# Moving the zeroing of the sine weights' first row (columns 0 to 1023) ahead of the mixing matrices' loads

## The chip, the cores and the metric

The kernel runs on one core of a Trainium2 chip. The time is that of the device for one execution, in microseconds (us). The program drives five engines, each with its own list of instructions that it works off in order: TensorE (PE, with a separate row PEld for its weight loads), VectorE (DVE), ScalarE (ACT), GpSimd (POOL) and SyncE (SP). SP computes nothing in this kernel: it issues transfers (DMAs), which then run on 16 DMA engines. An instruction that needs something from another engine, or from a transfer, waits on a semaphore, and everything behind it on its own engine waits too.

## The reference

The input x has 8 batches of 3008 positions with 256 values each. The reference takes the discrete Fourier transform over the positions and over the values, keeps the real part, and sends each of the 24064 rows through a small network with the activation h * sigmoid(1.702 h):

```
X = np.fft.fft(x, axis=1)
X = np.fft.fft(X, axis=2)
x = X.real.astype(np.float32).reshape(B * S, D)      # 24064 x 256
h = x @ w_in                                          # 256 x 2048
g = h * (1.0 / (1.0 + np.exp(-1.702 * h)))
return g @ w_out                                      # 2048 x 256
```

All of it is float32.

## The kernel before

**The mathematics.** 3008 is 47 times 64, so the transform over positions is done in two stages: 47 points (for batch 0 `mix_first`, later `mix1`) and then 64 points (`stage2`). The transform over the values is not done on the data at all. It is multiplied into w_in: `fold_w` makes a cosine version `wcs[0]` and a sine version `wcs[1]` of w_in, each 128 rows by 2048 columns. The sine of row 0 would be zero, and its place is used for something else: row 0 of `wcs[1]` first holds the weights of the highest frequency (the "Nyquist" row), which `first_row` copies into the small tiles `af1` and `af2`, 512 columns at a time.

**The slots.** The main loop has 384 slots and three more to drain it (loop variable `t`, line 978). Sixteen slots make a block, three blocks a batch, eight batches the run. A slot computes 256 of the hidden units for 256 positions and their mirror images. The first eight slots (`NP` is 8) form their products with `hidden(t)`, and `rows(t)` corrects the result for what row 0 of `wcs[1]` contributes. From slot 8 on another scheme is used: `middle(t)` (line 584) fills a PSUM bank with the Nyquist part, `begin(t)` adds the cosine product and `begin(t, 1)` the sine product into the same bank, and this is right only if row 0 of `wcs[1]` is zero by then. Slot t uses 256 of the 2048 columns, chosen by the last three bits of t: slots 0 to 3 and 8 to 11 use columns 0 to 1023, slots 4 to 7 and 12 to 15 the others.

**The zeroing.** `no_row(c0)` (line 497) is one DMA of 4 KB: it copies 1024 zeros from a table in DRAM into row 0 of `wcs[1]`, columns c0 to c0 + 1023. It is called twice: `no_row(0)` after `hidden(4)` in slot 4, and `no_row(1024)` after `hidden(7)` in slot 7. It may not overwrite the row before the last of the earlier products has read it: for columns 0 to 1023 that is `hidden(3)`.

**What SP has in its list around it.** SP's order is the order in which the Python code emits the calls. Work that is hung on a slot with `at(t, ...)` is emitted at the end of that slot. In slots 0 and 1 SP gets the last two loads of the raw w_out (`load_out`, line 397, 1 MB each). At the end of slot 3 come `load_matrices` (line 324, four loads of the 47-point matrices into `w1`), `turn` (lines 196 and 192, three DMAs that write the reversed half of the next x to the DRAM tensor `Xr1`), and `load_x` (line 205, eight loads of the next x into `xt`, half of them from `Xr1`). Then follow `no_row(0)` and `no_row(1024)`. The next things in the list are a small DMA to DRAM in slot 9 (line 383) and the first stores of results in slot 10 (line 815).

SP's DMAs signal on eight semaphores in turn, so a DMA is issued only when the one eight places ahead of it has landed. One DMA more or less in the list therefore changes which earlier DMA a later one waits for.

**The slots just after the first eight.** Slot 8 is the first in which `begin(t, 1)` reads the zeroed row. PE's order from there is: `begin(8, 1)`, a part of `product(5)`, `begin(9)`, the rest of `product(5)`, then `stage2` of block 1 (line 360), `begin(9, 1)`, a part of `product(6)`, `begin(10)`. The banks are shared: the results of slots 8 and 10 lie in bank `b0`, and `stage2` in slot 8 uses `b0` between the two. So `stage2` on PE waits until DVE has read slot 8's bank (`backward(8)`, line 557), and `middle(10)` on ACT waits until DVE has transposed `stage2`'s result out of `b0` (line 366). Two further groups of work lie in these slots: `small_weights(0)` to `(3)` on DVE (line 687, four instructions each, in slots 7 to 10), and on POOL the last `finish_out` (line 465), `differences` (line 475, four instructions each, in slots 5 to 8) and `sums` (lines 614 and 615). On DVE `small_weights(1)` stands in slot 8 after `backward(8)` and before the transposes of line 366. On ACT `forward(t)` is line 599, `doubled(t)` line 596 and `activate_back(t)` line 606.

From slot 11 on POOL also does `fold1` (lines 218 to 231) on the x that `load_x` brought.

Of the kernel before, what the change touches and what calls it, by code (L numbers as in the profile page):

```python
# [112 lines left out]
def kernel(ctx: ExitStack, tc, x, w_in, w_out, tab1, tab2, out):  # L113
# [255 lines left out]
    def nyquist(b, blk):  # L369

        nb = nbt[b, blk] = pqp.tile([128, 512], F32, tag="nb", name="nb")
        row = pqt[b, blk][0:1, 1, :]
        if (b, blk) != (0, 0):
            nc.sync.dma_start(out=nb[:], in_=view(Nd, (b * NBLK + blk) * 512, [0, 128], [1, 512]))
            return
        ps = bank("psn")
        halves(ps[:], ones[:], row, start=True, stop=True)
        nc.scalar.copy(nb[:], ps[:])
# [39 lines left out]
    def low_up(key, lo=0, n=1024):  # L418

        nc.scalar.activation(pre[key][2][:, lo:lo + n].bitcast(F32), raw[key][:, lo:lo + n, 0], ACTF.Copy, scale=2.0 ** -29,  # L420
                             bias=2.0 ** 23)

    def low_down(key, lo=0, n=1024):
        r = pre[key][2][:, lo:lo + n]
        nc.scalar.activation(r, r.bitcast(F32), ACTF.Copy, bias=-2.0 ** 23)

    def bounds(key, end=True):
        prepare(key)
        squares(key, nc.scalar)
        clamp(key)  # L430
        low_up(key)
        if end:
            low_down(key)
# [43 lines left out]
    def fold_w(n):  # L477
        ps = [bank("psw") for _ in range(2)]
        for i in range(2):
            for cs in range(2):  # L480
                halves(ps[cs][:], cd[:, i, cs, :], wst[n][:, i, :], start=(i == 0), stop=(i == 1))
        for cs in range(2):

            nc.scalar.copy(wcs[cs][:, n * 512:(n + 1) * 512].rearrange("p (f c) -> p f c", f=4),
                           free(ps[cs][:], 0, [1, 4], [4, 128]))

    def first_row(n):

        ps = bank("psf")
        for f in range(4 * n, 4 * n + 4):  # L490
            halves(ps[:, f:f + 1], wcs[1][0:1, f * 128:f * 128 + 128], twos[:], start=True, stop=True)
        nc.scalar.copy(af2[:, 4 * n:4 * n + 4], ps[:, 4 * n:4 * n + 4])
        nc.scalar.activation(af1[:, 4 * n:4 * n + 4], ps[:, 4 * n:4 * n + 4], ACTF.Copy, scale=0.5)


    def no_row(c0):
        nc.sync.dma_start(out=wcs[1][0:1, c0:c0 + 1024], in_=tab1[127:128, n0 + 4:n0 + 1028])
# [22 lines left out]
    def hidden(t):  # L520

        n = width(t)
        pa, pb = (bank(name, f"b{i}" if t == NP - 3 else None) for i, name in enumerate(("pa", "pb")))
        for ps, cs in ((pa, 0), (pb, 1)):
            for i in range(2):
                halves(ps[:, i * 256:i * 256 + n], *operands(t, cs, i), start=(i == 0), stop=(i == 1))
        v = sp.tile([128, 512], F32, tag="v", name="v")
        nc.scalar.copy(two(v[:], n), two(pa[:], n))
        vb[t] = v, pa, pb
# [43 lines left out]
    def activate(t):  # L573
        g = free(ht[t][:], 0, [256, 4], [1, width(t)])
        nc.scalar.activation(g, g, ACTF.Gelu_apprx_sigmoid)

    def middle(t):

        b, blk, hh, p = steps[t]
        n = width(t)  # L580
        x = xb[t] = bank("x", f"b{t % 2}")
        for i in range(2):
            f = 2 * p + i
            nc.scalar.activation(x[:, i * 256:i * 256 + n], nbt[b, blk][:, hh * 256:hh * 256 + n], ACTF.Copy,  # L584
                                 scale=af1[:, f:f + 1])

    def begin(t, cs=0):

        n = width(t)
        for i in range(2):  # L590
            halves(xb[t][:, i * 256:i * 256 + n], *operands(t, cs, i), start=False, stop=(cs == 1))

    def doubled(t):
        n = width(t)
        g = gt[t] = sp.tile([128, 512], F32, tag="v", name="g")
        nc.scalar.activation(two(g[:], n), two(xb[t][:], n), ACTF.Copy, scale=2.0)  # L596

    def forward(t):
        nc.scalar.activation(front(t), two(xb[t][:], width(t)), ACTF.Gelu_apprx_sigmoid)  # L599
# [180 lines left out]
    def swap(t):  # L780

        if not group_end(t):
            return
        n = width(t)
        one, two_, kept = (free(big[lo:lo + 64], RES + at, [512, 2], [1, n]) for lo, at in ((64, 0), (0, 256), (64, 1024)))
        nc.scalar.copy(kept, two_)
        nc.scalar.copy(two_, one)
        nc.scalar.copy(one, kept)
# [134 lines left out]
    def at(t, fn, *args):  # L923
        extra.setdefault(t, []).append((fn, args))
# [9 lines left out]
    rows_at = {1: 1, 4: 2, 6: 3}  # L934
    for t, c in ((0, 2), (1, 3)):
        at(t, load_out, c, nc.sync)
    at(3, load_matrices)
    if B > 1:
        for k in range(3):
# [38 lines left out]
    for t in range(n + LAG):  # L978
        if t < NP:
            if t == NP - 3:  # L980
                spare[:] = [tag for tag in spare if tag[0] == "o"] + ["b2"]
            if t == NP - 1:
                middle(NP)
            hidden(t)
            if t == NP - 1:
                begin(NP)
                no_row(1024)
            if t == 4:
                no_row(0)
            if t == 0:  # L990
                low_up(in2)
                nyquist(0, 0)
                low_down(in2)
            if t in rows_at:
                first_row(rows_at[t])
            if t >= LAG and t != LAG + 1:
                product(t - LAG, 0, None)
            if t == LAG:
                product(1, 0, None)
            if t == 5:  # L1000
                bounds(("out", 2))
            if t == 6:
                low_down(("out", 3))
            if t:
                activate(t - 1)
            if t == 3:
                bounds(("in", 3))
            if t == 5:
                bounds(("out", 3), False)
            if t in early:  # L1010
                fold_w(early[t])
            rows(t)
            if t == NP - 1:
                doubled(NP)
                middle(NP + 1)
        else:
            after, special = (any(fn in (mix1, stage2) for fn, _ in extra.get(k, ())) for k in (t - 1, t))
            if t < n:
                begin(t, 1)
            if t == NP:  # L1020
                activate(t - 1)
            if t < n:
                forward(t)
            if after and t + 1 < n:
                middle(t + 1)
            opening = (t - LAG) % NP == 0 and t >= NP + LAG
            one, other = (t - LAG, (1, 2, 4, 7)), (t - LAG - 1, (5, 6, 3))
            if opening:
                small_products(*other)
            cut = 0 if opening and not after else 3 if after else 2  # L1030
            product(t - LAG, 0, cut)
            if after:
                small_products(one[0], one[1][:1])
                small_products(other[0], () if opening else other[1][:1])
            if t + 1 < n:
                begin(t + 1)
            if not opening:
                small_products(other[0], other[1][after:])
            product(t - LAG, cut, 6 if t - LAG == last else None)
            small_products(one[0], one[1][after:])  # L1040
            swap(t - LAG - 2)
            if t < n:
                backward(t)
            if t + 1 < n:
                doubled(t + 1)
            if t < n:
                activate_back(t)
                sums(t, nc.gpsimd)
            if t + 2 < n and not special:
                middle(t + 2)  # L1050
            combine_small(t - LAG - 1)
            if t - LAG == last:
                product(last, 6, None)
            sums(t - 1, nc.vector)
            deeper(t - 2, 0)
            deeper(t - 3, 1)
        if t == NP:
            psu.close()
            low = ctx.enter_context(tc.tile_pool(name="low", bufs=1, space=PS))
            pot["low"] = low.tile([128, 3 * 512], F32, tag="low", name="low")  # L1060
        if t >= LAG:
            combine(t - LAG)
            combine_last(t - LAG - 2)
            turn_last(t - LAG - 3, 0)
            turn_last(t - LAG - 4, 1)
        if t >= NP:
            spare[:] = [f"b{t % 2}"] * special + ["b2"]
        for fn, args in extra.get(t, ()):
            fn(*args)
# [28 lines left out]
```

## Time and profile before

| What | Value |
|---|---|
| time, median of 3 runs | 1858.91 us (1858.37 to 1861.0) |
| the profiled execution: its time | 1863.36 us |
| the profiled execution: its span | 1861.6 us |
| PE busy | 1843.4 us, 99% of the span |
| DVE, ACT, POOL busy | 82%, 62%, 52% of the span |
| mean granted TensorE clock | 0.997 |
| DMA moved | 105.31 MB, 57 GB/s on average |

The span is the time from the first to the last instruction of the profiled execution; the time of that execution lies 1.76 us above it and holds what happens before and after. In a timeline each line has the start in us, the length in us, the engine, the line of the source, the operation, the tiles (written <- read), shapes and a count of merged instructions; in square brackets stands how long the engine was idle before it and what ended that. In a table of windows the columns after the stretch are its length, the busy time of each engine asked for with the number of instructions, then the granted clock of TensorE (1.00 is full speed), the share of DMA time and GB/s.

### The profile page before, as it was taken

The page shows a single profiled execution, that of the slowest core. Times are in us where ns is not written, and L with a number is a line of the kernel's source. Part 1 is how long each engine was busy: PE and PEld are TensorE (multiplying, and loading weights), DVE is VectorE, ACT ScalarE, POOL GpSimd, SP SyncE. Part 2 cuts the span into 40 slices and gives each one's busy share as a digit, 9 for nine tenths or more (in the row PEclk, how much of TensorE's full clock was granted, in tenths as well). Part 3 has the DMA queues.
Part 4 walks back from the last instruction along what each step waited for, and adds up shares of the span by engine and source line. Part 5 has one row for each costly group of instructions (what it writes and reads, how often), then busy time and mean ns, then how long its engine had stood idle before and what let it go on. Part 6 is the DMA issues. An engine that isn't in the chain of part 4 may idle for free.

```text
span 1861.6 us, 56078 instructions
## 1 busy us (share of the span) xinstructions
PE 1843.4 (99%) x23720; PEld 1403.2 (75%) x23720; DVE 1520.3 (82%) x2222; ACT 1145.5 (62%) x2240; POOL 971.5 (52%) x1053
## 2 busy tenths in 40 slices
PE   8999999999999999999999999999999999999998
PEld 4577777777777777777777777777777777778776
DVE  6878888888788877987789878888888888878874
ACT  5656665666566656666665666656666666656663
POOL 4777345844367443773347633486435754434442
PEclk9999999999999999999999999999999999999999
DMA  8721340224112250113302232031421111100111
GB/s 266 192 60 35 78 71 18 67 57 92 29 21 70 54 96 19 51 45 85 66 13 57 52 86 52 15 76 37 99 33 24 36 44 38 31 19 13 22 20 24
DMA packets 149691, 105.31 MB, mean 57 GB/s; under 512 B 106041, under 2 KB 130649, under 8 KB 148880
## 3 DMA queue, kind: packets, MB, share of 16 engines
q1 hardware_dynamic: 146608, 99.68, 23.6%
q8 instruction: 187, 3.06, 0.7%
q10 hardware_dynamic: 2832, 2.05, 0.4%
q14 instruction: 64, 0.52, 0.1%
HBM read 64.41 MB, written 48.05 MB: 60 GB/s over the span
## 4 chain that ended last, share of the span: by engine, by line
PE 91%; DVE 3%; POOL 2%; DMA 2%; ACT 1%; issue 1%; SPq 0%; DVEq 0%; POOLq 0%; ACTq 0%
PE x L184 33%; PE o L184 25%; PE low L677 24%; PE o L677 4%; PE ps L255 2%; PE ps L360 1%; DMA wcs<-in_tab_dram 1%; DVE big L643 1%; DMA xt<-in_x_dram 1%; ACT x L584 1%; DMA big<-in_moe_w_in_dram 0%; DVE big L778 0%; PE po L184 0%; PE psw L184 0%; POOL xt L227 0%
## 5 line engine op out<-in xcount | busy, mean ns | idle before, releaser
L614 POOL TENSOR_TENSOR big<-big 128x256 f32<-128x256 f32 (+1 forms) x376 | 347.5, 924 | 835.7 <-ACT big L606 724.3
L184 PE MATMUL x<-pq,wcs 128*64 128x256 f32 (+1 forms) x6016 | 772.3, 378 | 5.1 <-DMA wcs<-in_tab_dram 3.9
L643 DVE TENSOR_TENSOR big<-big 128x512 f32<-128x512 f32 (+1 forms) x736 | 624.2, 862 | 31.3 <-PE low L677 14.2
L184 PE MATMUL o<-big,wo 128*64 128x256 f32 (+1 forms) x4800 | 622.1, 376 | 0.0
L184 PEld LDWEIGHTS x<-pq,wcs 128*64 128x64 f32 x6016 | 410.4, 137 | 195.7 <-issue 19.3
L184 PEld LDWEIGHTS o<-big,wo 128*64 128x64 f32 x4800 | 342.2, 137 | 148.4 <-DVE big L621 0.5
L596 ACT ACTIVATE g<-x 128x512 f32<-128x512 f32 (+1 forms) x376 | 221.6, 589 | 375.0 <-PE x L184 373.7
L557 DVE TENSOR_TENSOR big<-g,x 128x512 f32<-128x512 f32 (+2 forms) x440 | 253.7, 588 | 198.4 <-ACT big L599 197.8
L677 PE MATMUL low<-big 128*64 128x128 f32 (+1 forms) x5888 | 382.9, 270 | 0.0
L584 ACT ACTIVATE x<-nb,af 128x256 f32<-128x256 f32 (+1 forms) x752 | 352.7, 469 | 12.2
L677 PEld LDWEIGHTS low<-big 128*64 128x64 f32 x5888 | 337.6, 137 | 29.2
L615 POOL TENSOR_TENSOR big<-big 128x256 f32<-128x256 f32 (+1 forms) x376 | 359.0, 955 | 0.0
L599 ACT ACTIVATE big<-x 128x512 f32<-128x512 f32 (+1 forms) x376 | 220.5, 586 | 201.9 <-PE x L184 168.5
L606 ACT ACTIVATE big<-big 128x512 f32<-128x512 f32 (+1 forms) x376 | 231.9, 617 | 40.5 <-DVE big L557 38.6
L677 PE MATMUL low<-big,wo 128*64 128x128 f32 (+1 forms) x2944 | 220.2, 270 | 0.1
L677 PEld LDWEIGHTS low<-big,wo 128*64 128x64 f32 x2944 | 171.6, 137 | 3.2 <-DVE big L643 0.4
L622 DVE TENSOR_TENSOR big<-big 128x512 f32<-128x512 f32 (+1 forms) x188 | 157.7, 839 | 6.5
L621 DVE TENSOR_TENSOR big<-big 128x512 f32<-128x512 f32 (+1 forms) x188 | 136.3, 725 | 5.5 <-POOL big L614 5.5
L778 DVE TENSOR_TENSOR big<-big,low 128x512 f32<-128x512 f32 (+3 forms) x184 | 109.1, 610 | 3.5
L677 PEld LDWEIGHTS o<-big,wo 128*64 128x64 f32 x1472 | 92.3, 137 | 24.9
L677 PE MATMUL o<-big,wo 128*64 128x128 f32 (+1 forms) x1472 | 110.0, 270 | 0.0
L227 POOL TENSOR_TENSOR xt<-xt 111x510 f32<-111x510 f32 x56 | 82.0, 1465 | 4.4
(95 smaller groups left out, 967.5 us busy)
## 6 DMA issues: line engine op xcount, KB each, us to landing
out_dram<-os SPq DMA_DIRECT2D x284, 64.0 KB
t<-Td SPq DMA_DIRECT2D x22, 512.0 KB
Td<-xt SPq DMA_DIRECT2D x56, 192.0 KB
xt<-in_x_dram SPq DMA_DIRECT2D x14, 512.0 KB
xt<-Xr SPq DMA_DIRECT2D x14, 512.0 KB
nb<-Nd SPq DMA_DIRECT2D x23, 256.0 KB
out_dram<-os SPq DMA_DIRECT2D x96, 56.0 KB
Xr<-in_x_dram SPq DMA_DIRECT2D x7, 752.0 KB
```

What stands on the lines that cost most here:

```text
L184: nc.tensor.matmul(out[c0:c0 + 64], lhsT=lhs[:, c0:c0 + 64], rhs=rhs, skip_group_check=True, **how)
L557: nc.vector.tensor_tensor(free(out, at + m - 1, [by, 2], [RUN, blocks], [-1, m]), *ins, op=op)
L584: nc.scalar.activation(x[:, i * 256:i * 256 + n], nbt[b, blk][:, hh * 256:hh * 256 + n], ACTF.Copy, scale=af1[:, f:f + 1])
L596: nc.scalar.activation(two(g[:], n), two(xb[t][:], n), ACTF.Copy, scale=2.0)
L599: nc.scalar.activation(front(t), two(xb[t][:], width(t)), ACTF.Gelu_apprx_sigmoid)
L606: nc.scalar.activation(back(t), back(t), ACTF.Gelu_apprx_sigmoid)
L614: eng.tensor_tensor(right(t, S1, n), left(t, A21, n), right(t, A22, n), op=ALU.add)
L615: eng.tensor_tensor(left(t, S3, n), left(t, A11, n), left(t, A21, n), op=ALU.subtract)
L621: eng.tensor_tensor(s2, s1, a11, op=ALU.subtract)
L622: eng.tensor_tensor(s4, a12, s2, op=ALU.subtract)
L643: nc.vector.tensor_tensor(out, i0, i1, op=how)
L677: nc.tensor.matmul(o, lhsT=lhs, rhs=rhs, start=first_in, stop=(p == NP - 2), skip_group_check=True)
```

## The change

The first `no_row` is emitted at the end of slot 3, as the first of what is hung on that slot, so on SP it stands just ahead of `load_matrices`. The call in slot 4, behind the eight loads of the next x, goes. The second, `no_row(1024)`, stays where it was.

```diff
     for t, c in ((0, 2), (1, 3)):
         at(t, load_out, c, nc.sync)
+    at(3, no_row, 0)
     at(3, load_matrices)
     if B > 1:
         for k in range(3):
             at(3, turn, 1, k)
         for k in range(4):
             at(3, load_x, 1, k)
...
             if t == NP - 1:
                 begin(NP)
                 no_row(1024)
-            if t == 4:
-                no_row(0)
             if t == 0:
                 low_up(in2)
```

The lists of PE, DVE, ACT and POOL keep their instructions and their order. On SP one DMA moves fifteen places forward. `no_row(0)` waits in both kernels for the last matmul of `hidden(3)`. Because of the eight semaphores in turn, the fifteen DMAs that it now stands ahead of each wait for the DMA one place later than before: `turn`'s second DMA for `load_out(2)`, its third for `load_out(3)`, and the first x load for `no_row(0)` itself. `begin(8, 1)` waits for `no_row(0)` in both.

## The prediction

> **What bounds the kernel now.** I read the page first. Its row of busy times says that PE has almost no idle time to give back:
>
> ```profile
> PE 1843.4 (99%) x23720; PEld 1403.2 (75%) x23720; DVE 1520.3 (82%) x2222; ACT 1145.5 (62%) x2240; POOL 971.5 (52%) x1053
> ```
>
> So a gain must be one of the few holes in PE. The chain of work that ended last, in order of time, has one piece that is no work (start, length, what):
>
> ```profile
> 71.22 0.64 PE pa L184 x5
> 71.86 15.00 DMA wcs<-in_tab_dram
> 86.86 0.14 issue
> 87.00 0.98 PE x L184 x8
> ```
>
> This is `no_row(0)`: issued at 71.86, landed at 86.86, and PE goes on at 87.00 with `begin(8, 1)`. PE's timeline shows what it cost there:
>
> ```profile
> 79.48 3.62 PE L184 MATMUL o<-big,wo 128*64 128x256 f32 x32
> 87.00 0.98 PE L184 MATMUL x<-pq,wcs 128*64 128x226 f32 x8 [3.89 <-DMA wcs<-in_tab_dram]
> 87.78 1.57 PE L184 MATMUL o<-big,wo 128*64 128x256 f32 x8
> 89.08 1.78 PE L184 MATMUL x<-pq,wcs 128*64 128x226 f32 x8
> 90.58 3.30 PE L184 MATMUL o<-big,wo 128*64 128x256 f32 x24
> 93.81 1.16 PE L360 MATMUL ps<-t,small 64*32 64x128 f32 x64
> ```
>
> The hole is 3.89 us, and what follows is slow: the second x group takes 1.78 us where 0.98 is usual. The windows table (PE busy, granted clock, DMA share, GB/s) says why:
>
> ```profile
> 87.00:88.00 1.00, 1.00 (x10) 1.00 0.02 8
> 88.00:89.00 1.00, 1.00 (x8) 0.60 0.00 0
> 89.00:90.00 1.00, 1.00 (x8) 0.50 0.06 16
> 91.00:92.00 1.00, 1.00 (x10) 0.70 0.00 0
> ```
>
> The clock falls after the hole and is back at 92. Last I read SP's timeline, for when the row could be sent:
>
> ```profile
> 43.65 7.09 SPq L397 DMA_DIRECT2D big<-in_moe_w_out_dram  x2
> 50.79 1.81 SPq L324 DMA_DIRECT2D w<-in_tab_dram  x4
> 56.55 0.66 SPq L192 DMA_DIRECT2D Xr<-in_x_dram  x1
> 61.41 0.35 SPq L205 DMA_DIRECT2D xt<-in_x_dram  x1
> 70.90 0.86 SPq L205 DMA_DIRECT2D xt<-Xr  x1
> 71.86 7.34 SPq L497 DMA_DIRECT2D wcs<-in_tab_dram  x2
> ```
>
> **What the Trainium skill says.** "TensorE: Matmul & The Clock Gate", What's actually happening: after an idle window of some 3.4 us the clock goes to half, and returns after about as long of work. The trace agrees: a hole of 3.89 us, then shares of 0.60, 0.50, 0.50 and 0.70. "DMA: Bandwidth & Descriptors", Queues, rings and completion order: all that SP issues shares one row of rings, one per DMA engine, and each ring is worked off in order. That fits 4 KB taking 15.00 us behind x loads. "SBUF — State Buffer", Who interferes with whom: a DVE instruction with two SBUF inputs contends with a POOL instruction that reads SBUF. The trace agrees, see below.
>
> **The change, part by part.**
>
> *The new place.* SP reaches it at 50.79, after the second L397, which waited 6.1 us for ACT. The wait of `no_row(0)` is for the last matmul of `hidden(3)`, whose `pb` group runs from 48.44 to 49.50 in PE's timeline: over by 1.3 us. So nothing queues behind it. It costs one issue, 0.29 us (the row of line 497: 234 to 350 ns), on SP.
>
> *Landing.* Ahead of it in the rings is what was ahead of the first x load: the last w_out load, which had landed by 61.41 (SP's first x load waited 4.1 us for it). I estimate 61 to 64. It is needed at 83.1, where the product before it ends (79.48 + 3.62). Some 20 us are spare, so the wait goes whole: 3.89 us.
>
> *The clock.* From 87.00 to the start of `begin(9, 1)` at 94.90, PE took 7.90 us. At full clock, by the pieces of the chain a little later: x 0.76 (100.50), o 0.86 (101.27), x 0.76, o of 24 at 0.108 each (20 in 2.16 at 98.34) 2.59, `stage2` 1.09, issue gaps 0.3: 6.3 us. So 1.6 us is clock; the windows give 0.40 + 0.50 + 0.50 + 0.30 = 1.7 us. I take 1.6, as the sum also holds the gaps. Together PE can be 5.5 us earlier at `begin(9, 1)`: at 89.4.
>
> *What becomes late next.* DVE and POOL had used the hole to catch up, and this is the term that I subtract:
>
> ```profile
> 83.23 1.37 DVE L687 TENSOR_TENSOR big<-wo,big 128x256 f32<-128x256 f32 x1
> 85.39 0.94 DVE L687 TENSOR_TENSOR big<-wo,big 128x256 f32<-128x256 f32 x1
> 89.72 0.43 DVE L687 TENSOR_TENSOR big<-wo,big 128x256 f32<-128x256 f32 x1
> 95.01 1.44 DVE L366 STREAM_TRANSPOSE pq<-ps 128x256 f32<-128x256 f32 x4 [4.19 <-PE ps L360]
> ```
>
> `small_weights` runs at 0.94 to 1.37 us an instruction while POOL is at lines 465 and 475 (to 87.59), and at 0.42 when POOL is idle (89.27 to 90.8). `small_weights(0)` still ends at 86.33. `backward(8)`, 0.69, then ends at 87.0, in time for `stage2`, which needs its bank at 88.3. `small_weights(1)` follows at once, and now POOL is not idle beside it: it finishes `differences(2)`, does `sums(8)` and begins `differences(3)`. At 0.94 each the four end at 90.8 rather than at 88.5. The transposes start then instead of at 89.4. The two that free `b0` (0.36 each) end at 91.5, and `middle(10)` starts at 91.5, where 96.38 - 5.5 = 90.9 would be PE's pace. Loss: 0.6 us, which PE waits at `begin(10)`. At 0.42 each nothing is lost; at 1.37 each the end is 92.5, `middle(10)` 93.2, the loss 2.3. After this DVE waits for ACT again (3.23 us idle at 101.89 before), so the lag ends there.
>
> *The fifteen DMAs moved behind.* Each starts 0.3 us later; `turn`'s third also waits for the last w_out load, 61.41 instead of 56.55, its second until about 56.5. The reversed x and the x loads may so end up to 5 us later than now: by about 92 instead of 87. POOL's first `fold1` stood at 110.86 and will stand at 106; 14 us cover it. SP's next item, `no_row(1024)`, waits for `hidden(7)` until 78.7 in both. It is needed by `begin(12, 1)`, after 100.
>
> *Whether it lasts.* From 109 to 130 POOL is nearly always busy (9.84 of 10 us from 120 to 130) and carries the chain. But it starts on PE's signal (idle 3.60 at 108.98), so it starts earlier too. Later loads and stores are issued on the progress of slots. Nothing in the chain is tied to a fixed time. Sum: 3.89 + 1.6 - 0.6 = 4.9 us.
>
> Against the profiled execution this is a span of 1856.7 and a time of 1858.5. That execution lies 4.45 us above the median, with the same program; I apply the difference to the median: 1858.91 - 4.9 = 1854.0.
>
> **The rivals.**
>
> *A second wait takes more of it.* If DVE and POOL hinder each other at the 1.37 us rate, 3.2 us remain: 1855.7. For it: POOL gets no pause between 81.6 and 93. Against it: three of four instructions in the same crowd took 0.94 or less. If they don't hinder each other at all: 5.5, 1853.4.
>
> *The gain is hidden.* The stretch from 110 to 149 is POOL's and DVE's. If something there had its own clock, as the x loads, PE would arrive early and wait: 1858.9. For it: POOL leads that part of the chain. Against it: POOL was idle over 3 us before each of slots 9, 10 and 11, with x already there.
>
> *Slower.* The x loads, pushed back through the semaphores, come too late for `fold1`. Price: 1 us for each us after the point where POOL wants them, 106; the old time is reached at 110.9, and slower by 0.2% (3.7 us) at 114.6: 1862.6. The delays that I can name give 92, so it needs over 20 us more, as from a pile-up in the DRAM to DRAM copies. Against it: the DMA share falls to 0.27 by 85:86, so there is room.
>
> *It doesn't do what it says.* The row could still land late. It would have to take 32 us from 50.8.
>
> **How the numbers follow.** A measurement of this kernel can tell about 0.2%, 3.7 us, from no change. The forecast's case (wait and clock loss gone, loss 0 to 1.2: 1853.4 to 1854.6, with the medians' scatter 1852.3 to 1855.2) has 0.79; the second wait 0.10, of which I count 0.06 as a gain above 3.7; hidden or no effect 0.06; slower 0.05. So faster 0.85, same 0.10, slower 0.05. The range 1852.0 to 1857.0 takes in the first two and leaves out the rest.
>
> **What would show it.** Right: no idle time at `begin(8, 1)`; clock 1.00 in all windows from 80 to 95; line 497 first issued near 50.8; the transposes of line 366 at 90 to 91; line 687's second group at some 0.9 us each; a short idle before `begin(10)` named ACT L584; POOL's first line 218 near 106, without a DMA before it. Wrong: PE idle at another place between 83 and 95 of a microsecond or more; POOL waiting for xt; the first L497 waiting for PE.

## The result, and the profile after

Over 21 timed runs each, taken in turn on one chip, the kernel after has a median of 1857.47 us (1856.12 to 1858.2) and the kernel before 1860.2 us (1858.19 to 1865.14). The ratio is 0.9982, 95% interval 0.9976 to 0.9989: a gain of 3.3 us, between 2.0 and 4.5 (the medians alone differ by 2.7). That is clear of zero but, at 0.18%, just inside the 0.2% that the prediction had called too little to tell. Two things stand out beside the medians. The kernel before scatters over 7 us and the kernel after over 2 us. And the two profiled executions differ by far more than the medians: spans of 1861.6 and 1855.1 us, times of 1863.36 and 1856.93 us.

The page of the kernel after, its row of busy times:

```profile
PE 1839.6 (99%) x23720; PEld 1400.0 (75%) x23720; DVE 1521.1 (82%) x2222; ACT 1146.3 (62%) x2240; POOL 971.9 (52%) x1053
```

PE is busy 3.8 us less than before with the same number of instructions. Half of that is the slow clock behind the gap: from the start of `begin(8)` to the start of `begin(9, 1)` PE is busy 12.29 us before and 10.38 after. The other half lies ahead of `begin(8)`, most of it in the first 40 us, before SP reaches the row in either kernel. The timeline of PE, kernel after, from the end of the first eight slots:

```profile
78.79 3.62 PE L184 MATMUL o<-big,wo 128*64 128x256 f32 x32
82.25 0.93 PE L184 MATMUL x<-pq,wcs 128*64 128x226 f32 x8
83.01 1.03 PE L184 MATMUL o<-big,wo 128*64 128x256 f32 x8
83.87 0.93 PE L184 MATMUL x<-pq,wcs 128*64 128x226 f32 x8
84.64 2.76 PE L184 MATMUL o<-big,wo 128*64 128x256 f32 x24
87.33 1.16 PE L360 MATMUL ps<-t,small 64*32 64x128 f32 x64
88.41 0.98 PE L184 MATMUL x<-pq,wcs 128*64 128x226 f32 x8
...
90.87 0.98 PE L184 MATMUL x<-pq,wcs 128*64 128x226 f32 x8 [0.18 <-ACT x L584]
```

The second line is `begin(8, 1)`: no idle time stands behind it, and the groups after it take 1.03, 0.93 and 2.76 us where they had taken 1.57, 1.78 and 3.30. The windows of the same stretch (PE busy, clock, DMA share, GB/s) stay at full clock:

```profile
83.00:84.00 1.00, 1.00 (x12) 1.00 0.99 100
...
87.00:88.00 1.00, 1.00 (x52) 1.00 0.00 0
```

SP's timeline shows the row in its new place, issued at 49.02:

```profile
43.14 5.68 SPq L397 DMA_DIRECT2D big<-in_moe_w_out_dram  x2
49.02 0.28 SPq L497 DMA_DIRECT2D wcs<-in_tab_dram  x1
49.36 1.69 SPq L324 DMA_DIRECT2D w<-in_tab_dram  x4
...
61.61 0.67 SPq L192 DMA_DIRECT2D Xr<-in_x_dram  x1
62.32 0.43 SPq L205 DMA_DIRECT2D xt<-in_x_dram  x1
...
71.10 0.86 SPq L205 DMA_DIRECT2D xt<-Xr  x1
78.28 0.24 SPq L497 DMA_DIRECT2D wcs<-in_tab_dram  x1
```

It did wait for PE there, though only some 0.2 us: SP was free at 48.82, and the last group of `hidden(3)` on PE runs from 47.93 to 48.99. The third DMA of `turn` (line 192) waits for the last w_out load as foreseen, 61.61 instead of 56.55. The last x load is still issued at 71.10, 0.2 us later than before.

Where the time came from can be cut in three. From the start of `begin(8)` to the start of `begin(9, 1)` PE took 94.90 - 78.72 = 16.18 us before and 88.41 - 78.03 = 10.38 after: 5.80 us. Up to `begin(8)` the two executions differ by 0.69. From `begin(9, 1)` to the end of the span it is 1861.6 - 94.90 = 1766.70 before and 1855.1 - 88.41 = 1766.69 after. So in this pair everything was gained at one place and nothing was given back. Why the medians then differ by only 3 us was the question for the experiments.

### The profile page after: what moved, and what is told of

It reads as the page before. It is cut to its first block, busy times and chain, and to the rows that moved or that the text cites. A ratio compares the mean times of both kernels' runs of the same rounds, so it can differ in the third digit from the quotient of the medians.

```text
span 1855.1 us, 56077 instructions
## 1 busy us (share of the span) xinstructions
PE 1839.6 (99%) x23720; PEld 1400.0 (75%) x23720; DVE 1521.1 (82%) x2222; ACT 1146.3 (62%) x2240; POOL 971.9 (52%) x1053
## 4 chain that ended last, share of the span: by engine, by line
PE 92%; DVE 2%; POOL 2%; ACT 1%; DMA 1%; issue 1%; SPq 0%; DVEq 0%; POOLq 0%; ACTq 0%
PE x L184 33%; PE o L184 26%; PE low L677 24%; PE o L677 4%; PE ps L255 2%; PE ps L360 1%; DVE big L643 1%; PE psw L184 1%; DMA xt<-in_x_dram 1%; ACT x L584 1%; DMA big<-in_moe_w_in_dram 0%; PE pa L184 0%; DVE big L778 0%; PE po L184 0%; PE pb L184 0%
```

## The experiments

**The theory** (A in the expectations): the row lands at a different time in each execution of the kernel before, and the loss of clock behind the gap comes whole or not at all; the profiled execution had both, a median one has less. **The rival** (B): every execution loses the 5.8 us, and the kernel after gives some back later, in executions other than the profiled one. Below, "excess" is the time from `begin(8)` to `begin(9, 1)` above the 10.38 us of the kernel after.

**Both kernels once more.** No edit.

> The kernel before, unchanged, against itself. Theory A (the gap at begin(8, 1) and the clock loss behind it differ from execution to execution; the profiled one had more than usual): ratio 1.000, single times spread over 5 us or more, and the profile shows a gap other than 3.89 us, with span minus (gap plus clock loss) again near 1856.1 (1861.6 - 3.89 - 1.6). Theory B (the gap is 3.9 us in every execution and the kernel after gives some of the gain back later, on other executions): a gap of 3.6 to 4.2 us again at a time near the median, 1859 to 1860.

> The kernel after, unchanged. Theory A: no gap, ratio 0.9975 to 0.999, times within 2 us of each other, and from the start of begin(9, 1) to the end 1766.7 us as in both profiles so far. Theory B: the stretch from begin(9, 1) to the end is longer than 1766.7 by 2 us or so in a typical execution.

Measured: the kernel before against itself has a ratio of 0.9998 (0.9990 to 1.0006), the kernel after against it 0.9984 (0.9978 to 0.9991), times from 1855.86 to 1858.16 us. PE's timeline of the new profile of the kernel before, span 1860.4:

```profile
78.02 0.93 PE L184 MATMUL x<-pq,wcs 128*64 128x226 f32 x8
...
85.71 0.98 PE L184 MATMUL x<-pq,wcs 128*64 128x226 f32 x8 [3.30 <-DMA wcs<-in_tab_dram]
86.49 1.62 PE L184 MATMUL o<-big,wo 128*64 128x256 f32 x8
...
93.61 0.98 PE L184 MATMUL x<-pq,wcs 128*64 128x226 f32 x8
```

A gap of 3.30 with the clock loss, in an execution of 1862.21 us; excess 15.59 - 10.38 = 5.21. That time isn't near the median, so this profile alone doesn't decide between A and B. From `begin(9, 1)` to the end it is 1766.79. Less the 5.21 the span is 1855.2; I had expected 1856.1. Of the difference 0.3 comes from having put the excess of the first profile at 5.5 instead of 5.80, and the rest from `begin(8)`, which starts 0.70 us earlier here. The kernel after again has 10.38 and 1766.78: no trace of B.

In the same series the kernel before was timed 65 times. 28 of these times lie between 1858.2 and 1859.4 and 19 between 1861.3 and 1862.6, with 7 from 1860.3 to 1861.2. In a later series of 55 the same stretches hold 20, 8 and 13, so two separate heaps are not a steady mark of this kernel. The mean granted clock, which is on record for every execution, averages 0.9983 over the 28 and 0.9973 over the 19; in the kernel after it is 0.9984. A mean lower by 0.0010 is 1.9 us of full-speed work over an execution. That fits a clock loss in the upper group and none in the lower, but it doesn't say at which place. So a fast execution had to be profiled too.

**Two more profiles of the kernel before.** No edit.

> The kernel before once more, for another profiled execution. Theory A: time = 1857.2 + gap + clock loss, with the clock loss 0 for a gap under some 2.5 us and 1.6 above, so a time near 1859 goes with a gap of 1 to 2.5 us at full clock and a time near 1862 with a gap of about 3 us and slow windows. Rival: a gap of 3 us or more also in an execution of 1859.

> As the look before it: time = 1857.2 + gap + clock loss, within 0.8 us.

The first took 1858.74 us. PE's timeline:

```profile
79.05 3.62 PE L184 MATMUL o<-big,wo 128*64 128x256 f32 x32
84.02 0.98 PE L184 MATMUL x<-pq,wcs 128*64 128x226 f32 x8 [1.35 <-DMA wcs<-in_tab_dram]
...
85.67 0.96 PE L184 MATMUL x<-pq,wcs 128*64 128x226 f32 x8
```

and the chain that ended last, same kernel and run:

```profile
69.87 14.02 DMA wcs<-in_tab_dram
83.89 0.14 issue
```

A gap of 1.35 us, and full speed at once after it. The second took 1860.1 us. PE's timeline and then its chain:

```profile
80.24 0.93 PE L184 MATMUL x<-pq,wcs 128*64 128x226 f32 x8
...
85.56 0.98 PE L184 MATMUL x<-pq,wcs 128*64 128x226 f32 x8 [0.93 <-DMA wcs<-in_tab_dram]
```

```profile
72.40 13.02 DMA wcs<-in_tab_dram
```

Only 0.93 us, at full clock. The rule 1857.2 + gap + clock loss gives 1858.55 (measured 1858.74) and 1858.1 (measured 1860.1): the second misses by 2.0, more than the 0.8 allowed. The reason is in its first line: `begin(8)` starts at 80.24 instead of near 78, so this execution had lost 2 us already before slot 8. Its trace shows where. From 20 to 24 us the granted clock was 0.63, against 0.96 to 1.00 in the other twelve profiles, and PE comes to its next `pa` group at 40.93 instead of 39.92 in the execution before it. The rest is a wait of 1.27 us for DVE at 47.5, where the execution before it waits 0.32. The scatter of the kernel before is therefore not the gap alone. From `begin(9, 1)` to the end the two took 1766.76 and 1766.52.

**A gap of a set length.** In the kernel after, ACT repeats `doubled(8)`, which `begin(8, 1)` has to wait for; each repeat writes the same values again. The number of repeats is 7, 9 and 12.

```diff
             if t == NP - 1:
                 doubled(NP)
+                for _ in range(7):
+                    nc.scalar.activation(two(gt[NP][:], width(NP)), two(xb[NP][:], width(NP)), ACTF.Copy, scale=2.0)
                 middle(NP + 1)
```

> The kernel after, with doubled(8) on ACT done seven more times, so that begin(8, 1) waits for ACT instead of for a transfer: a gap of a set length. At 0.57 us each the last ends near 83.6, a gap of about 1.2 us at 82.4. Theory A (the clock loss is all or nothing and needs a gap of some 2.5 us or more): clock 1.00 throughout, time 1857.3 + 1.2 = 1858.5. Rival (the clock loss grows with the gap, half of it or so): some windows under 1.00 already here, time 1859.

> The same with nine more: a gap of about 2.4 us. Theory A: near the edge, so the single times form two groups 1.6 us apart or lie wholly in one of them: 1859.7 without the clock loss, 1861.3 with it. Rival: one group near 1860.7.

> The same with twelve more: a gap of about 4.0 us. Theory A: clock 0.5 for some 3.4 us after the gap in every execution, time 1857.3 + 4.0 + 1.6 = 1862.9. Rival: 1857.3 + 4.0 + 2.0 = 1863.3 with a shorter or longer slow stretch than in the kernel before.

Medians: 1858.67, 1860.94 and 1862.78 us; ratios to the kernel before 0.9991 (0.9982 to 0.9999), 1.0003 (0.9995 to 1.0012) and 1.0015 (1.0008 to 1.0022). PE's timelines, with seven, nine and twelve repeats:

```profile
84.86 0.98 PE L184 MATMUL x<-pq,wcs 128*64 128x226 f32 x8 [1.32 <-ACT g L1015]
85.67 1.03 PE L184 MATMUL o<-big,wo 128*64 128x256 f32 x8
```

```profile
85.17 0.98 PE L184 MATMUL x<-pq,wcs 128*64 128x226 f32 x8 [2.48 <-ACT g L1015]
85.98 1.03 PE L184 MATMUL o<-big,wo 128*64 128x256 f32 x8
```

```profile
87.15 1.77 PE L184 MATMUL x<-pq,wcs 128*64 128x226 f32 x8 [4.22 <-ACT g L1015]
88.71 1.89 PE L184 MATMUL o<-big,wo 128*64 128x256 f32 x8
```

The next windows of the last one:

```profile
87.00:88.00 1.00, 0.85 (x6) 0.51 0.04 8
88.00:89.00 1.00, 1.00 (x8) 0.50 0.00 0
90.00:91.00 1.00, 1.00 (x10) 0.79 0.07 16
```

The gaps came out as set. The excess was 1.54 us for a gap of 1.32, 2.70 for 2.48 (both at full clock) and 6.05 for 4.22. So a gap costs its length plus 0.2 us, and once the clock falls 1.6 to 1.7 us more: 6.05 - 4.22 - 0.22 = 1.61 here, 5.21 - 3.30 - 0.22 = 1.69 and 5.80 - 3.89 - 0.22 = 1.69 in the two profiles of the kernel before that lost it. With nine repeats the single times run from 1858.90 to 1863.16, five up to 1860.23 and seven from 1860.87: wider than the other two, but without the clean split that was expected, and the median lies nearer to the rival's 1860.7 than to either of the two values of theory A. The mean granted clock over all runs was 0.9983, 0.9975 and 0.9972 with seven, nine and twelve repeats. So some executions with nine repeats probably lost the clock although the profiled one did not; without their profiles that is not shown.

**Work in the gap.** The kernel before, with six matmuls that nobody reads just ahead of `begin(8, 1)`.

```diff
+            if t == NP:
+                warm(6)
             if t < n:
                 begin(t, 1)
```

> The kernel before with six matmuls on data that nobody reads just ahead of begin(8, 1): 2.6 us of work in the gap. Theory A (the clock falls because PE is idle for some 3.4 us or more): clock 1.00 in all windows from 83 to 95, about 1.3 us of a gap like the profiled one left, ratio 0.999 (gain 1.6 us in executions that had the full gap, loss in those with a gap under 2.6). Rival (the clock falls for another reason, such as the transfers or the change of scheme at slot 8): windows at 0.5 to 0.7 as before, ratio 1.000.

The median is 1862.67 us, ratio 1.0011 (1.0004 to 1.0017). I had sized the filler wrongly. PE's timeline:

```profile
82.00 5.42 PE L330 MATMUL warm<-wcs 128*128 128x512 f32 x12
87.35 0.98 PE L184 MATMUL x<-pq,wcs 128*64 128x226 f32 x8
```

It is 5.4 us instead of 2.6 (the trace shows each of the six matmuls as two), longer than any gap in a profile, so the gain that was to be seen is buried. The clock is 1.00 in this profile, but that tests little. Nothing waited for the row, so its landing isn't recorded, and the transfers had ended early:

```profile
82.00:83.00 1.00, 1.00 (x5) 1.00 0.18 18
83.00:84.00 1.00, 1.00 (x4) 1.00 0.02 4
```

In the four profiles of the kernel before the row landed 0.4 to 0.9 us after the end of the last 1 us window ahead of it with a DMA share of 0.1 or more. An estimate from this is that it landed by 84 here, so that the gap would have been some 2 us at most and the clock might have stayed up anyway. What does speak for the theory is the scatter: with the gap filled by a constant, all 21 times lie within 2.3 us (1861.86 to 1864.12), as in the kernel after, and 1862.67 - 5.5 (the excess) is 1857.2, the kernel after.

**The row ahead of the last two x loads only.** The edit is shown against the kernel before.

```diff
         for k in range(4):
+            if k == 3:
+                at(3, no_row, 0)
             at(3, load_x, 1, k)
...
-            if t == 4:
-                no_row(0)
```

> no_row(0) stands ahead of the last two x loads (480 KB) instead of behind them. DMA moved 94 to 102 MB per ms, about 100 GB/s, at the end of the loads before, so 480 KB are 4.8 us. Theory A (the row's landing is set by what stands ahead of it in the rings): it lands 4 to 5 us earlier, at about 81, no gap or one under 0.5 us, clock 1.00, ratio 0.998 to 0.999, one group of times. Rival (only going ahead of all the loads helps): a gap of 2 us or more stays, ratio 1.000.

Median 1857.24 us, ratio 0.9985 (0.9979 to 0.9992), times from 1856.48 to 1858.48: the whole gain. SP's timeline and then PE's:

```profile
70.18 0.45 SPq L497 DMA_DIRECT2D wcs<-in_tab_dram  x1
70.67 0.33 SPq L205 DMA_DIRECT2D xt<-in_x_dram  x1
```

```profile
82.85 0.93 PE L184 MATMUL x<-pq,wcs 128*64 128x226 f32 x8
```

Issued at 70.18, about when the kernel before issues it (69.87 to 72.40), the row is there at 82.85, so within 12.7 us; how much earlier it landed isn't recorded. The DMA engines were still at work on the x loads then:

```profile
82.00:83.00 1.00, 1.00 (x12) 1.00 0.96 104
83.00:84.00 1.00, 1.00 (x14) 1.00 0.96 98
```

In the profiles of the kernel before the row landed only after these transfers had died down, for example at 83.89 with a DMA share of 0.25 from 82 to 83 and 0.00 from 83 to 84. So what made it late is what stood ahead of it in SP's order, and two places are enough; the engines need not run dry before it can land.

**The row on ACT's queue**, in slot 6 (`no_row` gets an engine, and ACT issues the first one).

> no_row(0) is issued by ACT in slot 6, some 73 us, with all eight x loads already issued by SP. Theory A (the row was late because it stood behind the x loads in SP's own rings): it lands within 4 us of its issue, no gap at begin(8, 1), clock 1.00, ratio like the kernel after, 0.998. Rival (it was late because the DMA engines were full, whoever issues): it lands at 84 to 88, a gap of 1 to 5 us stays, ratio 1.000. ACT loses one issue, 0.6 us, in slot 6, where it has idle time.

Median 1857.69 us, ratio 0.9986 (0.9980 to 0.9993), no gap, excess 0. But it doesn't tell the two apart. The build gave the eight semaphores out in another order, and SP's sixth x load came later, because it waited 9.5 us for the row itself. What line 497 did, and SP's timeline:

```profile
L497 ACTq DMA_DIRECT2D wcs<-in_tab_dram x1: 473/473/473, 71.5 to 71.5; - x1
```

```profile
66.94 0.55 SPq L205 DMA_DIRECT2D xt<-in_x_dram  x1
76.98 0.61 SPq L205 DMA_DIRECT2D xt<-Xr  x1
```

At 71.5 only five of the eight loads had been issued, so the row had fewer ahead of it anyway. It landed near 76.9, some 5.4 us after its issue and not within 4, when the transfers had run out: the DMA share is 0.93 from 75 to 76 and 0.05 from 76 to 77. So busy engines may delay the row on ACT's queue too, and whether that queue would have helped with all eight loads ahead is left open.

**More ahead of the row.** The kernel before, with one more transfer of 752 KB (`turn(7, 0)`, early; its bytes are written again later) between the x loads and `no_row(0)`.

> The kernel before with one more transfer of 752 KB from DRAM to DRAM on SP between the x loads and no_row(0). Theory A (what stands ahead in the rings sets the landing): at 100 to 200 GB/s 3.8 to 7.5 us later, a gap of 6 to 11 us, the clock loss the same 1.6 us or up to twice that, so 1864.8 to 1871.4, ratio 1.0025 to 1.006. Rival (the landing is set by something else, such as a wait of SP): gap of about 3 us as before, ratio 1.000.

Median 1862.02 us (1859.0 to 1863.49), ratio 1.0007 (0.9998 to 1.0016). The direction of the times is that of theory A, but the interval holds zero and the size is missed. PE's timeline and the windows of its one profile, an execution of 1859.83 us:

```profile
85.12 0.98 PE L184 MATMUL x<-pq,wcs 128*64 128x226 f32 x8 [2.93 <-DMA wcs<-in_tab_dram]
85.91 1.06 PE L184 MATMUL o<-big,wo 128*64 128x256 f32 x8
```

```profile
81.00:82.00 1.00, 1.00 (x12) 1.00 1.01 109
82.00:83.00 1.00, 0.19 (x2) 1.00 0.99 259
83.00:84.00 1.00, 0.00 (x0) 1.00 0.91 323
```

The x loads crawl at about 100 GB/s to the end, but the added transfer then runs at some 300, so an estimate of its cost is 2.5 us and not 3.8 to 7.5. Yet the row took 14.99 us from its issue, no longer than in two profiles of the kernel before (15.00 and 15.04). So this experiment doesn't show that more ahead makes the row later; it only doesn't contradict it. The gap of 2.93 us left the clock alone.

## Why the prediction was right or wrong

- **The wait goes, and no new one takes its place: right.** `begin(8, 1)` starts without idle time, and the row lands in time in both profiles of the kernel after. One of the signs that were named for being wrong did show: the row waited for PE, since SP reached it at 48.82 and not at 50.79. The wait was 0.2 us and cost nothing. The x loads, which might have ended up to 5 us later, did not: from 85 to 86 the DMA share is 0.07, and was 0.27 before.
- **The clock: right in mechanism and size.** 1.6 us was taken, 1.6 to 1.7 measured (three profiles), and without the gap it is gone. The condition was too strict: a gap of 3.30 us lost the clock too, shorter than the idle window of some 3.4 us that was reckoned with.
- **DVE and POOL in each other's way: the mechanism shows, the term was too large.** DVE's timeline in the kernel after:

```profile
86.02 0.41 DVE L687 TENSOR_TENSOR big<-wo 128x256 f32<-128x256 f32 x1
86.46 0.84 DVE L687 TENSOR_TENSOR big<-wo,big 128x256 f32<-128x256 f32 x1
...
88.84 1.43 DVE L366 STREAM_TRANSPOSE pq<-ps 128x256 f32<-128x256 f32 x4
```

  The second group of line 687 did slow down (0.41, 0.84, 0.89, 0.88 against 0.42 each), but the first of the four escaped. The transposes start at 88.84, 0.4 us after `stage2`'s end on PE. The half that frees `b0` is over near 89.6, and ACT reaches `middle(10)` at 89.89 anyway. The idle time before `begin(10)` is 0.18 us in both kernels: loss 0, not 0.6.
- **The sum for the profiled execution: too small, mostly by that term.** 4.9 was forecast; the place gave 5.80 (3.89 + 0.22 + 1.69). Of the 0.9 us 0.6 is the term and 0.3 is what gap and clock together gave above the 5.5 taken.
- **Moving the difference to the median: this step failed.** The prediction noted that the profiled execution lay 4.45 us above the median and took its gap off the median all the same. The gap is what differs between the executions: 3.89 and 3.30 us with the clock loss, 1.35 and 0.93 without, excess 5.80, 5.21, 1.57 and 1.16. A median execution can't lose 5.8 us at a place that cost it less. The mean of these four is 3.4, and the measured gain 3.3. Four are few, and the agreement is closer than they warrant. Set against the kernel after of the same series, the times from 1858.2 to 1859.4 lie some 2 us up and those from 1861.3 to 1862.6 some 5.
- **It lasts: right.** From `begin(9, 1)` to the end the thirteen profiles of this study take 1766.2 to 1767.1 us, whatever the kernel. The rivals that had the gain hidden or turned into a loss by late x loads didn't happen: in the kernel after, POOL reaches line 218 at 104.38 with no transfer to wait for.
- **The numbers.** The forecast gain of 4.9 us lies above the interval of 2.0 to 4.5. Applied to the 1858.91 us of the runs shown, the measured ratio gives 1855.6, inside the range of 1852.0 to 1857.0. That is partly luck. The case that was expected reached only to 1855.2, and the rest of the range was there for a second wait, which didn't come. The 0.6 us wrongly subtracted also brought the forecast nearer to the measured gain. And by the prediction's own measure of 3.7 us a gain of 3.3 is too little to tell, an outcome that it had given 0.10. The median of the 21 runs, 1857.47, is above the range, because the kernel before too was slower in that series, 1860.2.

Left open is why the row takes 13.0, 14.0 or 15.0 us from its issue in different executions, and why the clock stayed low until after 20 us in the execution that reached slot 8 some 2 us late. The profiles show that both happen, not their cause.

## What to carry to other kernels

A small transfer that somebody waits for should not stand behind bulk loads in the same issuing order: 4 KB took 13 to 15 us here, and two places further forward were enough. When the profiled execution is well above the median of the same program, suspect the very wait that you are pricing, and profile more than one execution before taking its length as the gain. A gap in PE has a price of its own once it is long enough to lower the clock, here 1.6 to 1.7 us: it pays to bring it under that length even where it can't be closed.

## What the runs showed of the hardware

In the profiles, one for each length, gaps of 0.93, 1.32, 1.35, 2.48 and 2.93 us left TensorE's clock at 1.00, and gaps of 3.30, 3.89 and 4.22 us were each followed by some 3.4 us at half clock, which cost 1.6 to 1.7 us in all three. The times with nine repeats suggest that a gap near 2.5 us may lower the clock in some executions. The drop can come late: 1.2 us after work had resumed in the first profile of the kernel before, and at once with twelve repeats.

At the end of the x loads the DMA engines were shown as fully busy at only about 100 GB/s (a share of 1.01 and 109 GB/s with the added transfer still to come), while the added DRAM to DRAM transfer behind them reached 323 GB/s at a share of 0.91. So a full DMA row in the page said little here about how many bytes move. A transfer that stood ahead of two loads landed while they were still moving 98 to 104 GB/s; behind them it landed after they had died down.
